# Top-k merge steps on TensorE moved to the front of their slot's tail and one slot later

## The chip, the cores and the metric

The kernel runs on one core of one Trainium2 chip. The metric is the device time of one execution in microseconds (us). The engines are named as in the profile: PE (TensorE, the matrix engine), PEld (its weight loads), DVE (VectorE), ACT (ScalarE), POOL (GpSimd) and SP (SyncE, which here issues transfers).

## The reference

The kernel computes attention with normalised queries and keys, then a mixture-of-experts layer in which each expert keeps at most its 80 best tokens.

```
q_n, k_n = rmsnorm(q, g_q), rmsnorm(k, g_k)      # q, k, v: 8 x 12 x 448 x 64
attn = softmax(q_n @ k_n.T / 8) ; x = (attn @ v) reshaped to 3584 x 768
probs = softmax(x @ w_gate)                      # 8 experts, one chosen per token
for e in experts:
    tokens = the (at most 80) tokens of expert e with the largest gate weight
    out[tokens] = gate_w * (relu(x[tokens] @ w1[e]) @ w2[e])   # others: zero
```

## The kernel before

**Tiling.** The 12 heads of a batch element are taken four at a time, so there are 24 groups of four heads, three to each of the eight batch elements b = 0 to 7. A group has seven rounds. One round is a score step (function `score`, L312: eight PE instructions, sixteen in the profile, into a PSUM tile `ps`), an exponential on ACT (L315, `ps` to `at`), and an attention-times-value step (`av`, L327, `at` into `po`). DVE adds up the seven `at` tiles of a group (`presum`, L339 and L341, tile `sm`).

**Order.** The order on every engine is written out by hand: the tile framework places semaphores and buffers, but moves nothing. Two rounds form a slot, and 84 slots (0 to 83) hold the attention. Each slot is emitted as: `begins`, the scores of two rounds, the presums of the two rounds before, `mid`, the AV steps of the two rounds before, then `end`. `begins`, `mid` and `end` are lists per slot, filled by `at_slot`, which appends. Every engine works through its own instructions strictly in that order.

**What else stands in a slot.** `end` holds the transposes of the next groups' normalised q and k (`transp`, L288, PE tile `tp`, copied by ACT in L300 and L302), the transposes of finished outputs (`xout`, L581, tile `xp`, copied by ACT into the single buffer `xb` in L586, then written to DRAM by SP in L593 and L594), and `rstd`. For q or k of a group, `rstd` is a DVE sum (L252) and scaling (L254) into `ms`, then a power on POOL (L261, `rs`). `normalise` in `mid` is POOL's multiplication L276 into `qn`, which `transp` reads. POOL also issues the staging copies of the expert weights (L175, L180).

**The merge.** When the three groups of a batch element are done, its gate is computed (L379 to L455), and then `merge` folds its 448 tokens into the running lists of the 80 best per expert, in six steps. Each step has PE work into a scratch tile `mp`, an ACT copy out of it, and mostly DVE work on the copy: `row` (L470, copy L474, then compares `beat`, L480 and L483), `experts` (L497, copy L501, more compares, `tied` L488 and L491), `own` (L506, copy L510, then `ahead` L514 and `cnt` L518), `counts` (L525 to L529, copies `back` L532 and `move` L534, then the chain `rnk`, `rank`, `put`, `keep`, L539 to L549), `place` (L557 and L561, copy L563) and `turn` (L567, copy L570). Batch elements 0 to 6 have a merge; the last one is handled behind the attention in its own code. The slot of a merge is given from b0 = (3b+2)*7//2, which is 7, 17, 28, 38, 49, 59 and 70.

**The buffers that matter.** `ps` and `mp` take turns in one pool of two PSUM buffers, so a merge step makes the next slot's second score step wait until ACT has copied `mp`:

```
scps = ps_stack.enter_context(tc.tile_pool(name="sc_ps", bufs=2, space=PSUM))
...
return scps.tile([128, 2, 512 if dt == F32 else 1024], dt, tag="sc", name="mp")
```

Of the kernel before, what the change touches and what calls it, by code (L numbers as in the profile page):

```python
# [20 lines left out]
def kernel(  # L21
# [15 lines left out]
    B, H, S, D = q.shape  # L37
# [168 lines left out]
    with av_stack:  # L206
# [406 lines left out]
        begins, mid, end = {}, {}, {}  # L613

        def at_slot(where, s, f, *a):
            where.setdefault(s, []).append((f, a))
# [9 lines left out]
        for g in range(NG):  # L626
            b0 = g * RD // 2
# [9 lines left out]
            for a in range(2):  # L637
                for f in range(2):
                    t = b0 - 4 + 2 * a + f
# [7 lines left out]
        for b in range(B):  # L647
            b0 = (NQ * b + NQ - 1) * RD // 2
            if b == B - 1:
                at_slot(end, b0 + 3, zl, b, range(NQ - 1))  # L650
                at_slot(end, b0 + 4, zl, b, range(NQ - 1, NQ))
                at_slot(end, b0 + 4, gate1, b)
                at_slot(end, b0 + 5, gate1t, b)
                at_slot(mid, b0 + 6, gate1v, b)
                continue
            at_slot(end, b0 + 5, zl, b, range(NQ))
            at_slot(end, b0 + 5, gate1, b)
            at_slot(end, b0 + 6, gate1t, b)
            at_slot(mid, b0 + 7, gate1v, b)
            at_slot(end, b0 + 7, gate2, b)  # L660
            at_slot(end, b0 + 7, gate2x, b)
            at_slot(mid, b0 + 8, gate2b, b)
            at_slot(mid, b0 + 8, gate2i, b)
            at_slot(mid, b0 + 8, gate2p, b)
            for t, fs in enumerate(merge(b)):
                for f in fs:
                    at_slot(end, b0 + 8 + t, f)
        at_slot(begins, 0, load_wgs)
        at_slot(end, NS - 3, weights_early)
        at_slot(end, NS, weights_late)  # L670
# [49 lines left out]
    b = B - 1  # L720
# [201 lines left out]
```

## Time and profile before

| what | value |
|---|---|
| median of three runs | 502.95 us (501.95 to 503.85) |
| the profiled execution itself | 498.67 us |
| its span, first to last instruction | 496.9 us |
| PE busy | 451.0 us, 91% |
| DVE busy | 358.0 us, 72% |
| ACT busy | 315.7 us, 64% |
| POOL busy | 267.7 us, 54% |
| mean granted PE clock | 0.978 of full speed |

The profile is of one execution, which was 4.28 us shorter than the median of the timed runs. Busy shares are means over a start of some 15 us, an attention of some 410 us and an expert stage of some 70 us, so they don't say which engine holds up the work at a given moment; for that one reads what an engine waited for, and where. A number in square brackets at the end of a row of a timeline is the idle time of that engine just before the row, with the instruction that ended it. The profile merges neighbouring rows of one kind and counts each fp32 matmul of 448 columns as two.

### The profile page before, as it was taken

To read this page: it belongs to the slowest core of one execution; us is meant where nothing else is said; L and a number is where in the kernel's file an instruction comes from. 1 tells how busy PE (TensorE), PEld (TensorE's weight loads), DVE (VectorE), ACT (ScalarE), POOL (GpSimd) and SP (SyncE) were. 2 spreads that over 40 slices of the span, in tenths; PEclk is the share of its full clock that TensorE was granted. 3 is DMA by queue.
4 is the path that set the end of the run, shared out by engine and by line. 5 is a ranking of instruction groups with operands and counts; after the bars stand their busy time and mean duration, and the time that the engine had idled before them with its cause. 6 is when DMAs were issued, how large, how long until landed. Compare 5 with 4: busy or idle time off the path is not lost. (4 is left out here: it accounts for less than half of the span.)

```text
span 496.9 us, 11200 instructions
## 1 busy us (share of the span) xinstructions
PE 451.0 (91%) x4527; PEld 222.3 (45%) x4527; DVE 358.0 (72%) x567; ACT 315.7 (64%) x491; POOL 267.7 (54%) x199
## 2 busy tenths in 40 slices
PE   6889999999899999699899999998998999869890
PEld 5334444353434444344344444443443444558770
DVE  4688756997899758776699669966976767445530
ACT  4777867877677768565787678767776666302210
POOL 2497883676555938618538835774578210242221
PEclk9799999999999999899999999999999999989996
DMA  6369979596958994994597959788939947779922
GB/s 217 117 136 300 254 184 251 97 291 183 243 121 222 230 256 74 267 162 159 172 167 247 254 166 241 188 218 200 238 98 220 211 90 264 281 214 354 372 98 60
DMA packets 68435, 100.84 MB, mean 203 GB/s; under 512 B 8480, under 2 KB 60192, under 8 KB 67104
## 3 DMA queue, kind: packets, MB, share of 16 engines
q1 hardware_dynamic: 52160, 70.54, 45.0%
q0 software_dynamic: 15616, 29.13, 32.9%
q8 instruction: 35, 0.57, 0.4%
q10 hardware_dynamic: 608, 0.46, 0.3%
q14 instruction: 16, 0.13, 0.1%
HBM read 101.12 MB, written 39.90 MB: 284 GB/s over the span
## 5 line engine op out<-in xcount | busy, mean ns | idle before, releaser
L261 POOL TENSOR_TENSOR rs<-ms,nhalf 128x14 f32<-128x14 f32 x46 | 136.5, 2970 | 130.2 <-DVE ms L254 124.0
L341 DVE TENSOR_TENSOR sm<-sm,at 128x896 f32<-128x896 f32 x120 | 155.6, 1297 | 24.1 <-ACT at L315 17.8
L315 ACT ACTIVATE at<-ps 128x896 f32<-128x896 f32 x168 | 147.8, 921 | 23.6 <-PE ps L312 19.2
L312 PE MATMUL ps<-qkT 64*64 64x448 f32 x1344 | 152.9, 561 | 9.6 <-ACT row L474 4.6
L327 PE MATMUL po<-at,vt 64*64 64x448 f32 x1344 | 145.4, 542 | 3.2 <-ACT us L332 3.2
L276 POOL TENSOR_TENSOR qn<-qk,rs 128x896 f32<-128x896 f32 (+1 forms) x45 | 84.5, 1894 | 8.3 <-DVE rs L267 8.2
L327 PEld LDWEIGHTS po<-at,vt 64*64 64x64 f32 x1344 | 50.2, 134 | 76.9 <-issue 67.0
L252 DVE TENSOR_REDUCE ms<-sq 128x14 f32<-128x896 f32 (+1 forms) x50 | 52.2, 1045 | 44.6 <-ACT sq L243 41.6
L312 PEld LDWEIGHTS ps<-qkT 64*64 64x64 f32 x1344 | 42.1, 134 | 73.7 <-issue 36.6
L288 PE MATMUL tp<-ident,qn 128*128 128x128 f32 x336 | 52.7, 280 | 5.1 <-DVE qn L276 3.5
L288 PEld LDWEIGHTS tp<-ident,qn 128*128 128x128 f32 x336 | 37.6, 142 | 32.0 <-issue 15.4
L586 ACT COPY xb<-xp 128x512 f32<-128x512 f32 x48 | 28.2, 588 | 36.6 <-PE xp L581 27.2
L243 ACT ACTIVATE sq<-qk 128x896 f32<-128x896 f32 (+1 forms) x50 | 45.9, 922 | 3.6 <-DMA qk<-in_k_dram 3.6
L581 PEld LDWEIGHTS xp<-ident,us 128*128 128x128 f32 x192 | 20.1, 140 | 34.7 <-issue 27.0
L300 ACT ACTIVATE qkT<-tp,gqk 128x512 f32<-128x512 f32 (+1 forms) x48 | 30.8, 643 | 4.7 <-PE tp L288 4.2
L302 ACT COPY qkT<-tp 128x384 f32<-128x384 f32 (+1 forms) x47 | 25.3, 538 | 12.0 <-PE tp L288 11.9
L581 PE MATMUL xp<-ident,us 128*128 128x128 f32 x192 | 31.5, 287 | 1.1 <-ACT xb L586 1.1
L863 ACT ACTIVATE h_sb<-ph 128x320 bf16<-128x320 f32 x16 | 7.0, 437 | 31.1 <-PE ph L859 31.1
L480 DVE TENSOR_SCALAR beat<-row,rg 128x128 bf16<-128x128 f32 (+3 forms) x28 | 23.2, 830 | 4.2 <-ACT row L474 3.8
L882 POOL DMA_INDIRECT out_dram<-yo,idxT x8 | 7.7, 963 | 34.2 <-DVE yo L877 14.9
L339 DVE TENSOR_TENSOR sm<-at 128x896 f32<-128x896 f32 x24 | 26.0, 1084 | 0.1
L332 ACT COPY us<-po 128x896 f32<-128x896 f32 x24 | 21.6, 902 | 5.8 <-PE po L327 5.8
(159 smaller groups left out, 407.9 us busy)
## 6 DMA issues: line engine op xcount, KB each, us to landing
wb_scratch<-in_moe_w_dram POOLq DMA_DIRECT2D x10, 1536.0 KB, 13.2
w_sb<-wb_scratch SPq DMA_DIRECT2D x10, 1536.0 KB, 11.1
vt<-in_v_dram SPq DMA_DIRECT2D x24, 448.0 KB, 6.1
out_dram<-zeros SPq DMA_DIRECT2D x28, 384.0 KB, 8.5
qk<-in_q_dram SPq DMA_DIRECT2D x23, 448.0 KB, 7.2
qk<-in_k_dram SPq DMA_DIRECT2D x23, 448.0 KB, 7.9
w_sb<-in_moe_w_dram POOLq DMA_DIRECT2D x6, 1536.0 KB, 15.3
xr_scratch<-xb SPq DMA_DIRECT2D x48, 192.0 KB, 5.5
```

The source lines that it names most:

```text
L243: nc.scalar.activation(st[g]["sq%d" % a][:, lo:hi], st[g]["qk"][a][:, lo:hi], AF.Square)
L252: nc.vector.reduce_sum(out=ms[:, lo:hi], in_=st[g]["sq%d" % a][:, lo:hi], axis=AX.X)
L261: nc.gpsimd.tensor_tensor(rs[:, lo:hi], ms[:, lo:hi], nhalf[:, lo:hi], op=ALU.pow)
L276: eng.tensor_mul(qn[:].rearrange("p (x hh) d -> p hh x d", hh=2)[:, h0:h1], qk[:, lo:hi].rearrange("p (hh x) d -> p hh x d", x=NX), rs[:, ...
L288: nc.tensor.transpose(tp[:, x * 128:(x + 1) * 128], qn[:, 2 * (x0 + x):2 * (x0 + x) + 2].rearrange("p h d -> p (h d)"), ident[:, :])
L300: nc.scalar.activation(o, i, AF.Copy, scale=gqk[:, :])
L312: nc.tensor.matmul(ps[u * 64:u * 64 + 64, hh, :S], T1[d, u, x * 64:(x + 1) * 64], T0[d, u, :], start=True, stop=True)
L315: nc.scalar.activation(at[:], ps[:, :, :S], AF.Exp)
L327: nc.tensor.matmul(po[hh * D:(hh + 1) * D, u, :S], vt[p, hh * NX + x, :], at[p, hh, :], start=(x == 0), stop=(x == RD - 1))
L341: nc.vector.tensor_add(s["sm"][:], s["sm"][:], s["at%d" % x][:])
L581: nc.tensor.transpose(xp[:, j * 128:(j + 1) * 128], us[:, u, c:c + 128], ident[:, :])
L586: nc.scalar.copy(xb[:, :, u * 128:(u + 1) * 128], xp[:, :].rearrange("p (j d) -> p j d", d=128))
```

## The change

For batch elements 0 to 5 each merge step goes to slot b0+9+t in place of b0+8+t, and it is put at the head of that slot's `end` list in place of its foot. The two or three parts of a step keep their order among themselves. The merge of batch element 6 stays as it was.

```
             for t, fs in enumerate(merge(b)):
-                for f in fs:
-                    at_slot(end, b0 + 8 + t, f)
+
+                ready = b < B - 2
+                for f in (reversed(fs) if ready else fs):
+                    if ready:
+                        end.setdefault(b0 + 9 + t, []).insert(0, (f, ()))
+                    else:
+                        at_slot(end, b0 + 8 + t, f)
```

On PE, around slots 15 and 16 (batch element 0), `row` (L470) stood between two slots, behind the output and q/k transposes:

```order
L327 MATMUL po<-at,vt 64x448 x8
L581 MATMUL xp<-ident,us 128x128 x4
L288 MATMUL tp<-ident,qn 128x128 x4
L470 MATMUL mp<-ident,rg 128x128 x4
L312 MATMUL ps<-qkT 64x448 x8
L327 MATMUL po<-at,vt 64x448 x8
L581 MATMUL xp<-ident,us 128x128 x4
L288 MATMUL tp<-ident,qn 128x128 x3
```

The same stretch of PE with the change:

```order
L327 MATMUL po<-at,vt 64x448 x8
L581 MATMUL xp<-ident,us 128x128 x4
L288 MATMUL tp<-ident,qn 128x128 x4
L312 MATMUL ps<-qkT 64x448 x8
L327 MATMUL po<-at,vt 64x448 x8
L470 MATMUL mp<-ident,rg 128x128 x4
L581 MATMUL xp<-ident,us 128x128 x4
L288 MATMUL tp<-ident,qn 128x128 x3
```

The step has moved behind a whole slot's scores and AV, and in front of that slot's transposes.

On DVE, at slots 18 and 19, where the chain behind `counts` stands; before:

```order
L341 TENSOR_TENSOR sm<-sm,at 128x896
L252 TENSOR_REDUCE ms<-sq 128x14
L254 TENSOR_SCALAR ms<-ms 128x14
L539 TENSOR_TENSOR rnk<-back,eq 128x32
L541 TENSOR_REDUCE rank<-rnk 128x4
L542 SCALAR_TENSOR_TENSOR rank<-rank,cnt 128x4
L545 TENSOR_TENSOR put<-iota,rank 128x320
L549 TENSOR_TENSOR keep<-iota,move 80x640
L339 TENSOR_TENSOR sm<-at 128x896
```

The same work on DVE with the change:

```order
L252 TENSOR_REDUCE ms<-sq 128x14
L254 TENSOR_SCALAR ms<-ms 128x14
L339 TENSOR_TENSOR sm<-at 128x896
L341 TENSOR_TENSOR sm<-sm,at 128x896
L539 TENSOR_TENSOR rnk<-back,eq 128x32
L541 TENSOR_REDUCE rank<-rnk 128x4
L542 SCALAR_TENSOR_TENSOR rank<-rank,cnt 128x4
L545 TENSOR_TENSOR put<-iota,rank 128x320
L549 TENSOR_TENSOR keep<-iota,move 80x640
```

Between the scaling of `ms` (L254), on which POOL's power waits, and the chain from `rnk` to `keep` there are now two presums. The orders of SP's and POOL's instructions are the same before and after.

## Rows read from the trace of the kernel before

**Rows 1.** Waits of PE: engine, tile, line, releaser: us in total, times, longest.
```profile
PE ps L312 <- ACT row L474: 4.6, 6, 0.9
PE ps L312 <- ACT move L534: 4.2, 2, 4.0
```

**Rows 2.** Timeline of PE, batch element 0: start, us, engine, line, instruction.
```profile
86.09 0.62 PE L470 MATMUL mp<-ident,rg 128*128 128x128 f32 x4 [0.17 <-DVE eqb L431]
86.64 0.98 PE L312 MATMUL ps<-qkT 64*64 64x448 f32 x8
88.49 0.98 PE L312 MATMUL ps<-qkT 64*64 64x448 f32 x8 [0.87 <-ACT row L474]
89.30 1.68 PE L327 MATMUL po<-at,vt 64*64 64x448 f32 x16
...
92.15 1.92 PE L312 MATMUL ps<-qkT 64*64 64x448 f32 x16
93.89 1.68 PE L327 MATMUL po<-at,vt 64*64 64x448 f32 x16
...
100.32 0.24 PE L525 MATMUL mp<-eqb,beat 128*128 128x8 bf16 x4
...
101.46 1.86 PE L312 MATMUL ps<-qkT 64*64 64x448 f32 x16
...
106.21 1.74 PE L312 MATMUL ps<-qkT 64*64 64x448 f32 x16
107.76 1.68 PE L327 MATMUL po<-at,vt 64*64 64x448 f32 x16
109.38 0.98 PE L288 MATMUL tp<-ident,qn 128*128 128x128 f32 x7
```

**Rows 3.** Timeline of PE, batch element 1.
```profile
138.10 0.98 PE L312 MATMUL ps<-qkT 64*64 64x448 f32 x8 [0.65 <-ACT row L474]
...
163.05 0.66 PE L288 MATMUL tp<-ident,qn 128*128 128x128 f32 x4
```

**Rows 4.** Timeline of DVE, batch element 0.
```profile
93.36 2.57 DVE L483 TENSOR_SCALAR beat<-row,rg 128x64 bf16<-128x64 f32 x1
...
101.60 1.08 DVE L341 TENSOR_TENSOR sm<-sm,at 128x896 f32<-128x896 f32 x1
...
103.71 0.17 DVE L254 TENSOR_SCALAR ms<-ms 128x14 f32<-128x14 f32 x1
...
104.43 0.49 DVE L545 TENSOR_TENSOR put<-iota,rank 128x320 bf16<-128x320 f32 x1
104.84 0.81 DVE L549 TENSOR_TENSOR keep<-iota,move 80x640 bf16<-80x640 f32 x1
```

**Rows 5.** Timeline of POOL, batch element 0.
```profile
103.96 2.59 POOL L261 TENSOR_TENSOR rs<-ms,nhalf 128x14 f32<-128x14 f32 x1 [0.33 <-DVE ms L254]
106.52 1.69 POOL L276 TENSOR_TENSOR qn<-qk,rs 128x896 f32<-128x896 f32 x1
```

**Rows 6.** Timeline of POOL, batch element 1.
```profile
157.48 3.36 POOL L261 TENSOR_TENSOR rs<-ms,nhalf 128x14 f32<-128x14 f32 x1 [1.37 <-PE ps L312]
160.81 1.68 POOL L276 TENSOR_TENSOR qn<-qk,rs 128x896 f32<-128x896 f32 x1
```

**Rows 7.** Timeline of PE, batch element 2.
```profile
208.41 1.76 PE L312 MATMUL ps<-qkT 64*64 64x448 f32 x8 [4.03 <-ACT move L534]
```

**Rows 8.** Timeline of ACT, batch element 2.
```profile
207.06 0.58 ACT L586 COPY xb<-xp 128x512 f32<-128x512 f32 x1 [4.12 <-DMA xr_scratch<-xb]
```

**Rows 9.** Timeline of SP and of POOL, batch element 2: issues of transfers.
```profile
194.41 1.48 SPq L593 DMA_DIRECT2D xr_scratch<-xb  x2
...
193.23 0.90 POOL L180 DMA_DIRECT2D wb_scratch<-in_moe_w_dram  x1
```

**Rows 10.** Busy time in windows (us), PE, PEld, DVE, ACT, POOL, granted clock, DMA.
```profile
208.40:211.00 2.60, 2.59 (x16) 1.08 (x20) 2.50 (x4) 1.55 (x2) 2.60 (x3) 0.52 0.70 251
```

**Rows 11.** Timeline of DVE, batch element 2.
```profile
210.19 1.94 DVE L545 TENSOR_TENSOR put<-iota,rank 128x320 bf16<-128x320 f32 x1
```

## The prediction

> **What bounds the kernel now.** I read the busy shares first (PE 91%, no other engine over 72%), then what PE waited for, then timelines around the longest of those waits. The list of PE's waits is headed by score steps that wait for a merge step's ACT copy: 4.6 us in six waits for `row`, 4.2 us in two for `move` [rows 1]. The reader is to see that there are six of the first kind, one per merge of batch elements 0 to 5, and that one single wait makes up nearly all of the second. The timelines alternate by batch element: the even ones (0, 2, 4) wait 0.87 us [rows 2], the odd ones (1, 3, 5) 0.65 us [rows 3]. Outside these places PE works through the slots of the attention almost without a pause, so what is taken off PE there is taken off the time, unless another engine then arrives late. The engine to watch is POOL: its multiplication `qn` feeds the q/k transposes, and it lies behind DVE's `ms`, on the engine where the merge's DVE parts stand.
>
> **The waits that go.** A pair of score steps normally takes 1.55 us to the AV steps behind it (107.76 − 106.21). In the slot behind `row` it takes 2.66 us (89.30 − 86.64), 1.11 us more, and behind `experts` 1.74 us (93.89 − 92.15), 0.19 us more [rows 2]. The cause is the pair of buffers that `ps` and `mp` share: with the step at the foot of a slot, its copy stands on ACT behind the slot's `xb` and `qkT` copies, and the second score step needs that buffer. At the head of `end` the copy stands in front of those two, and PE still has the transposes and one score step to do before it needs the buffer. I therefore take these waits as gone. For an even batch element that is 0.17 (`row` waiting for DVE) + 1.11 + 0.19 + about 0.15 for `counts`, an estimate from the 0.19: 1.6 us. For an odd one it is 0.65 + 0.24 (the part of 1.11 that the profile doesn't book as waiting) + 0.19 + twice 0.15 for `own` and `counts`: 1.4 us. PE's own instructions are the same ones, so they cost nothing new. The six slots' copies on ACT are only reordered; ACT's exponentials lie beside PE's AV and transposes.
>
> **What limits the gain.** PE can run ahead only as far as `qn` allows. Even: POOL's first `qn` ends at 106.52 + 1.69 = 108.21 [rows 5], and the four transposes that read it are the last four of the seven that start at 109.38, so about 109.8 [rows 2]: 1.6 us of slack. Odd: 160.81 + 1.68 = 162.49 [rows 6] against 163.05 [rows 3]: 0.56 us.
>
> How does that chain move? Up to the second scaling of `ms` in question the same instructions stand on DVE in both orders, since each compare, presum and reduction only changes places with its neighbour; DVE is busy there without a pause, so its sum stays. Three things differ:
> - POOL's power took 2.59 us when small operations of the merge followed the scaling on DVE [rows 5], and 3.36 us when presums followed [rows 6]. The new order puts presums there in the even elements: 0.77 us later. In the odd ones presums stand there already: 0.
> - In the even elements the chain from `rnk` to `keep` now stands behind two presums. From 103.79, right behind the start of the scaling [rows 4], two presums of 1.1 us and 0.64 us of `rnk` and `rank` (104.43 − 103.79) lead to `put` 2.85 us later, `keep` 3.26 us later and `keep`'s end 4.07 us later (0.41 = 104.84 − 104.43, and 0.81). The power ends 3.36 + 0.17 = 3.53 us after that point, so `qn` finds `keep` running and starts 0.5 us late.
> - In the old order compares were caught behind POOL's multiplications; the worst took 2.57 us [rows 4], some 2.2 us more than a compare that isn't caught. In the new one the compares start one slot later, and a presum and a compare meet the same multiplications, for 1.69 us each at most. Laying the rows end to end by hand I get DVE 0.8 us earlier in the even and 0.4 us earlier in the odd elements; the bounds are 0 and 2.2 us.
>
> Even: 1.6 − 0.77 − 0.5 + 0.8 = 1.1 us of room, less than the 1.6 saved; I take 1.0 for semaphores on the way. Odd: 0.56 + 0.4 = 0.96, less than 1.4; I take 0.9. Without the third point it is 0.3 and 0.56, with more of it the full 1.6 and 1.4. So the regular part is 3 × 1.0 + 3 × 0.9 = 5.7 us, bounds 2.6 and 9.0. `ahead`, `put` and `keep` come in time for their PE steps by my replay, by 0 to 1 us: if DVE is that much later, PE waits there instead of at the transposes, within the same bounds.
>
> **The one long stall.** In batch element 2 ACT's copy into `xb` waited 4.12 us for the previous group's write [rows 8]: issued at 194.41, 1.2 us behind a staging copy of weights [rows 9], it had landed only at 207.06. PE waited 4.03 us [rows 7], for the `move` copy queued behind `xb` on ACT, and then ran 2.6 us at half clock, 0.52 of full speed [rows 10], 1.2 GHz in place of 2.4, which cost about 1.3 us more. Price: 5.3 us. With the change PE has, at that point, one more score step and two AV steps that need nothing of ACT; it stops only at `counts`, for a buffer whose exponential stands behind `xb` on ACT. If the write takes the same 207.06 − 194.41 = 12.65 us from an issue 1.3 us earlier (0.17 + 1.11 saved by then), ACT resumes at 205.8 and PE at about 207.7, behind `xb`, `qkT` and one exponential (an estimate of 1.9 us). That is 0.7 us earlier than 208.41, with a score step of 0.78 (half of 1.55), AV steps of 1.62 (109.38 − 107.76) and 1.3 us of slow clock behind it, but `counts`, some 1.0 us (101.46 − 100.32 = 1.14, a little waiting in it), ahead of it [rows 2]: 0.7 + 0.78 + 1.62 + 1.3 − 1.0 = 3.4 us, of which 1.0 is counted as regular. That leaves 2.4 us, or 1.1 if the clock falls again; 5.3 if the write lands in time, for which it speaks that POOL's staging copy is now issued behind it (the power in front of it takes 0.77 us more). I take 2.4, since the only row of this transfer is that of 12.65 us.
>
> **Sum.** 5.7 + 2.4 = 8.1 us off the profiled execution (498.67 us, span 496.9 us). The timed median is 4.28 us above that execution for a reason that the profile can't show; I carry the difference over unchanged: 502.95 − 8.1 = 494.85, say 494.8 us. Own range of this case: 2.6 + 1.1 = 3.7 to 9.0 + 5.3 = 14.3 us, so 488.7 to 499.2 us.
>
> **Rivals.**
> - POOL's chain takes it all. The waits on `row` go, but the transposes wait for `qn` as long as the merge's DVE work comes a slot later, and the stall stays, because earlier PE work only reaches the write of `xb` sooner. For it speak the slack of 0.56 us; against it that in the even elements there are 1.6 us. It gives 0 to 3 us: 501.5 us.
> - Slower: `put` and `keep` land behind POOL's two multiplications in the even elements. Where that happened, `put` took 1.94 us in place of 0.49 [rows 11, 4]. If `qn` starts first, `put` waits out one multiplication and `keep` the second, 1.69 us each plus their own 0.41 and 0.81, so `keep` ends 4.6 us after `put`'s issue, some 4 us after PE wants it for `place`, which is now at the head of `end` with the transposes behind it. Against 1.6 us gained by then an even element loses 2.4 us. Three of them cost 7.2, the odd ones still give 2.7, the stall nothing: 4.5 us slower, 507.5 us. It decides by what comes first: `put` at 2.85 and `keep` at 3.26 us against `qn` at 3.53. With a power of 2.59 us, `qn` would start at 2.76 and win. That a presum follows the scaling is what speaks against it. The Trainium skill says in "SBUF — State Buffer", Who interferes with whom, that a VectorE instruction with two SBUF inputs and a GpSimd instruction that reads SBUF exclude each other, whichever is issued first holding the port to its end. By that rule this rival is the outcome if the order of issue tips; the trace agrees with the rule in the 1.94 us.
> - Everything goes: no chain binds and the `xb` write lands in time, 14.3 us: 488.7 us. For it speaks only that the staging copy moves behind the write.
>
> **How the numbers follow.** Forecast 0.55, everything goes 0.14, POOL's chain takes it all 0.18, slower 0.13. About 0.5% (2.5 us) is what a measurement of this kernel tells from no change. Faster: 0.55 + 0.14 and a quarter of the third case, some 0.74. Same: the rest of that case, 0.14. Slower: 0.12. The range 489.5 to 503.0 us leaves out the slower case and the far end of the all-goes case, and holds the third whole.
>
> **What would show it.** Right: no PE wait for `row` but for batch element 6; score steps of 1.55 us behind each merge step; the odd elements' transposes waiting some 0.5 us for `qn` on POOL; POOL's powers of 3.36 us in the even elements. Wrong: PE waiting at `place` (L557, L561) for `put` or `keep`, or at `counts` for `ahead`, or a stall of 3 us or more behind an `xb` copy in places where there was none; or a `row` wait that survives, which would say that ACT, not the place in the queue, was late.

## The result, and the profile after

The changed kernel takes 490.79 us (median of 4 runs, 490.19 to 491.93) against 503.4 us before (4 runs, 501.95 to 504.59): a ratio of 0.9753, 95% interval 0.9721 to 0.9786. The forecast was 494.8 us. The profiled execution took 490.89 us, its span is 489.0 us, 7.9 us less than the span before.

In the page of the changed kernel, the first line of part 1 gives busy time, share of the span and instructions. PE's busy time is 3.2 us less and POOL's 18.2 us more, though both issue the same instructions as before.

```profile
PE 447.8 (92%) x4527; PEld 224.5 (46%) x4527; DVE 353.7 (72%) x567; ACT 314.6 (64%) x491; POOL 285.9 (58%) x199
```

The list of PE's waits, to be held against [rows 1]:

```profile
PE tp L288 <- POOL qn L276: 8.0, 9, 2.5
...
PE mp L525 <- ACT at L315: 0.4, 1, 0.4
...
PE ps L312 <- ACT own L510: 0.2, 1, 0.2
```

Both rows of [rows 1] are gone: no score step waits for `row` or `move` any more. In their place the q/k transposes wait for POOL's `qn`. One of the nine waits, the longest (2.5 us), lies at the start of the program; eight, 5.5 us together, lie beside the merges.

In the timelines of PE a row of L312 marked x16 is the two score steps of a slot (one score step is four PE instructions, eight in the profile). The timeline of PE for batch element 0, against [rows 2]; the score steps behind `row` (L470) take 94.00 − 92.44 = 1.56 us, where it was 2.66:

```profile
91.10 0.65 PE L470 MATMUL mp<-ident,rg 128*128 128x128 f32 x4
...
92.44 1.73 PE L312 MATMUL ps<-qkT 64*64 64x448 f32 x16
94.00 1.68 PE L327 MATMUL po<-at,vt 64*64 64x448 f32 x16
...
109.10 0.33 PE L557 MATMUL mp<-info,put 128*80 128x40 bf16 x4
109.28 0.46 PE L561 MATMUL mp<-listn,keep 80*80 80x5 bf16 x8
109.59 0.53 PE L288 MATMUL tp<-ident,qn 128*128 128x128 f32 x3
111.44 0.66 PE L288 MATMUL tp<-ident,qn 128*128 128x128 f32 x4 [1.32 <-POOL qn L276]
```

`place` (L557, L561) waits for nothing; the four transposes behind it stand 1.32 us for `qn`. Where that comes from is to be read on POOL and DVE, first the timeline of POOL (against [rows 5]), then that of DVE (against [rows 4]):

```profile
101.87 3.39 POOL L261 TENSOR_TENSOR rs<-ms,nhalf 128x14 f32<-128x14 f32 x1 [3.10 <-DVE ms L254]
...
105.23 3.14 POOL L261 TENSOR_TENSOR rs<-ms,nhalf 128x14 f32<-128x14 f32 x1
108.35 3.04 POOL L276 TENSOR_TENSOR qn<-qk,rs 128x896 f32<-128x896 f32 x1
```

```profile
104.76 0.17 DVE L254 TENSOR_SCALAR ms<-ms 128x14 f32<-128x14 f32 x1
104.84 1.08 DVE L339 TENSOR_TENSOR sm<-at 128x896 f32<-128x896 f32 x1
105.96 1.09 DVE L341 TENSOR_TENSOR sm<-sm,at 128x896 f32<-128x896 f32 x1
...
107.61 0.49 DVE L545 TENSOR_TENSOR put<-iota,rank 128x320 bf16<-128x320 f32 x1
108.02 0.81 DVE L549 TENSOR_TENSOR keep<-iota,move 80x640 bf16<-80x640 f32 x1
108.76 1.08 DVE L341 TENSOR_TENSOR sm<-sm,at 128x896 f32<-128x896 f32 x1
```

`qn` takes 3.04 us where it took 1.69. It is issued at 108.35, while `keep` runs (to 108.83). Counted back from its end, 108.35 + 3.04 − 1.69 = 109.70, it got going only about when the presum behind `keep` was done (108.76 + 1.08 = 109.84). So two DVE instructions in a row went ahead of it, one of them issued after it. This is so all nine times that it meets `keep` and a presum in three profiles of the new order (after, after_again and a_xb2: 3.04 to 3.11 us).

It is not so behind every pair. Earlier in the same merge a multiplication met two presums, of which the first ran until 94.57; here it got in behind the first, and the second one, issued 0.69 us after it, stood for it (2.46 us in place of 1.08). POOL, then DVE:

```profile
93.92 2.20 POOL L276 TENSOR_TENSOR qn<-qk,rs 128x896 f32<-128x896 f32 x1
...
94.61 2.46 DVE L341 TENSOR_TENSOR sm<-sm,at 128x896 f32<-128x896 f32 x1
```

The rows show one difference: the second presum reads the `sm` that the first writes, and starts 0.04 us behind its end, while the presum behind `keep` reads nothing of `keep` and starts 0.07 us before its end (108.76 against 108.83). Whether that decides it was not tried.

The second place to look is ACT's wait for the write of `xb`, from the list of ACT's waits. Before:

```profile
ACT xb L586 <- DMA xr_scratch<-xb: 7.4, 2, 4.1
```

and after:

```profile
ACT xb L586 <- DMA xr_scratch<-xb: 1.3, 1, 1.3
```

There had been two stalls and not one: besides that of [rows 8] another of 3.3 us in the slots of batch element 6. Both are gone; the 1.3 us are at another place, in batch element 4. The timelines of SP and POOL for batch element 2 in the changed kernel show the issue of the write and that of the staging copy, against [rows 9]:

```profile
193.93 1.24 SPq L593 DMA_DIRECT2D xr_scratch<-xb  x2
...
194.88 0.91 POOL L180 DMA_DIRECT2D wb_scratch<-in_moe_w_dram  x1
```

The staging copy now stands 0.95 us behind the write, where it stood 1.2 us ahead of it, and the next copy into `xb` waits for no transfer.

**Where the time went.** The merges of the first six batch elements lie in slots b0+8 to b0+14. This table gives the time from the first score step of slot b0+8 to that of slot b0+15, as read from PE's timeline of each kernel (from the third on they are those of the experiments), with the sum over the six:

```
us, merge of batch element      0     1     2     3     4     5     sum
before                       32.47 33.00 38.04 32.92 32.11 33.19  201.73
after                        32.07 32.11 32.51 31.88 32.01 32.91  193.49
after, profiled again        32.07 32.10 34.20 31.88 32.00 32.92  195.17
before, second xb buffer     32.43 33.07 32.18 32.92 32.11 32.93  195.64
after, second xb buffer      33.83 32.18 32.58 31.94 32.08 32.98  195.59
after, earlier qn            31.13 31.77 31.07 31.77 30.91 32.04  188.69
before, both edits           32.81 32.93 32.10 32.93 32.11 32.93  195.81
after, both edits            31.19 31.78 31.14 31.78 30.30 31.78  187.97
```

Between the two profiles the merges give 8.24 us, of it 38.04 − 32.51 = 5.53 in element 2 alone, and slot 75 (the stall of element 6) 9.99 − 7.63 = 2.36 us. Against this the changed execution began its first score step 2.35 us later (17.05 us for 14.70); the rest is within 0.7 us. The two sums of the new order that stand near 195.6 (profiled again, and second xb buffer) each hold one merge that is 1.7 us longer (34.20 and 33.83), in which TensorE's clock fell behind a short wait; the last section shows it.

### The profile page after: what moved, and what is told of

Same layout as the page of the kernel before. It is cut to its first block, busy times and chain, and to the rows that moved or that the text cites. A ratio compares the mean times of both kernels' runs of the same rounds, so it can differ in the third digit from the quotient of the medians.

```text
span 489.0 us, 11182 instructions
## 1 busy us (share of the span) xinstructions
PE 447.8 (92%) x4527; PEld 224.5 (46%) x4527; DVE 353.7 (72%) x567; ACT 314.6 (64%) x491; POOL 285.9 (58%) x199
## 5 line engine op out<-in xcount | busy, mean ns | idle before, releaser
L261 POOL TENSOR_TENSOR rs<-ms,nhalf 128x14 f32<-128x14 f32 x46 | 146.5, 3188 | 104.8 <-DVE ms L254 100.6
L341 DVE TENSOR_TENSOR sm<-sm,at 128x896 f32<-128x896 f32 x120 | 169.0, 1408 | 22.2 <-ACT at L315 16.5
L315 ACT ACTIVATE at<-ps 128x896 f32<-128x896 f32 x168 | 145.7, 922 | 17.4 <-PE ps L312 17.4
L312 PE MATMUL ps<-qkT 64*64 64x448 f32 x1344 | 147.8, 553 | 1.1 <-DVE qkT L298 0.9
L276 POOL TENSOR_TENSOR qn<-qk,rs 128x896 f32<-128x896 f32 (+1 forms) x45 | 92.1, 2062 | 10.2 <-DVE rs L267 10.1
L312 PEld LDWEIGHTS ps<-qkT 64*64 64x64 f32 x1344 | 43.8, 133 | 62.3 <-issue 44.2
L879 PE MATMUL py<-w_sb,h_sb 128*80 128x384 bf16 x128 | 23.1, 332 | 1.8 <-ACT h_sb L868 1.8
```

Of the source, the lines that this page charges most:

```text
L261: nc.gpsimd.tensor_tensor(rs[:, lo:hi], ms[:, lo:hi], nhalf[:, lo:hi], op=ALU.pow)
L276: eng.tensor_mul(qn[:].rearrange("p (x hh) d -> p hh x d", hh=2)[:, h0:h1], qk[:, lo:hi].rearrange("p (hh x) d -> p hh x d", x=NX), rs[:, ...
L312: nc.tensor.matmul(ps[u * 64:u * 64 + 64, hh, :S], T1[d, u, x * 64:(x + 1) * 64], T0[d, u, :], start=True, stop=True)
L315: nc.scalar.activation(at[:], ps[:, :, :S], AF.Exp)
L341: nc.vector.tensor_add(s["sm"][:], s["sm"][:], s["at%d" % x][:])
```

## Experiments

The theory after this reading: nearly all of the gain is ACT's stalls behind the single `xb` buffer, which the new order happens to avoid; the merge's new place itself gives little, because the waits it saves come back as waits for `qn`. The rival: the gain is the saved `row` and `counts` waits, as most of the forecast's sum had it. The runs fall into three groups, each with its own runs of the kernel before: 500.17 us (25 runs) for the first four, 500.82 us (13 runs) for the next four, 501.27 us (11 runs) for the last three.

**again: the kernel before, unchanged.**

```
(no edit)
```

> The kernel before, unchanged, to see why its timed runs are 4 to 5 us longer than the profiled one (498.67 us) while the changed kernel's timed and profiled runs agree (490.8 and 490.89 us). First theory: the time is lost in stalls of ACT behind the write of xb, which vary from run to run; then this profile, if it is at about 503 us, shows three or four xb copies that waited 2 us or more for a transfer, against two (7.4 us in total) in the profile shown, and the same waits for row (4.6 us in six). Rival: the loss is spread, at the start or in the expert stage, and the xb waits are the same two.

Measured: 499.97 us (496.5 to 504.03), ratio 0.9989 (0.9949 to 1.0029). The list of ACT's waits:

```profile
ACT xb L586 <- DMA xr_scratch<-xb: 6.3, 2, 3.4
```

The stalls come back at the same two places, with other lengths (2.9 and 3.4 us). This profiled execution took 500.69 us, 2.0 us more than the first one, with 1.1 us less of waits for the write: these two profiles do not bear out that the stalls make the spread. The kernel before spreads over 6.6 us in 24 of these 25 runs (496.6 to 503.16; one took 504.62), the changed one over 1.7 in its four.

**head: the merge steps at the head of `end`, but in their old slot.**

```
-                        end.setdefault(b0 + 9 + t, []).insert(0, (f, ()))
+                        end.setdefault(b0 + 8 + t, []).insert(0, (f, ()))
```

> One part of the change alone: the merge steps of batch elements 0 to 5 go to the head of their slot's end list, but stay in their old slot (b0+8+t). First theory (both parts are needed, the slot later makes the operands ready): the waits of 0.87 and 0.65 us on the row copy go, but PE waits about 1.2 us at L470 for DVE's rg and eqb, and the merge's DVE work now stands ahead of rstd, so the transposes wait for qn some 1 to 2 us more per merge: 498 to 505 us, no gain. Rival (the place in the slot is all that counts): 491 to 494 us.

Measured: 498.64 us (496.83 to 500.5), ratio 0.9976 (0.9951 to 1.0001). PE's waits:

```profile
PE tp L288 <- POOL qn L276: 10.1, 9, 2.3
...
PE mp L470 <- DVE eqb L431: 2.4, 2, 1.2
```

The head of the list alone removes the `row` waits and both stalls (ACT has no wait for the write), but `row` now comes before the gate's DVE work is done, and the transposes wait longer. The merges take 202.08 us in sum: 6.4 us over the 195.64 of the old order without stalls (second xb buffer in the table), so what the stalls give is lost again there. The first theory held, in the time and in the wait of 1.2 us at L470.

**later: one slot later, at the foot.**

```
-                    at_slot(end, b0 + 8 + t, f)
+                    at_slot(end, b0 + 8 + t + (b < B - 2), f)
```

> The other part alone: the merge steps of batch elements 0 to 5 go one slot later (b0+9+t), but stay at the foot of their slot's end list. First theory (the place on ACT behind xb and qkT is what makes row wait, and the slot later alone only removes the 0.17 us wait of L470): row still makes the second score step wait 0.65 to 0.87 us six times, and the xb stall in batch element 2 stays or not by the timing of its transfer: 499 to 503 us. Rival (the slot later is what helps): 491 to 495 us, without the row waits.

Measured: 499.95 us (498.19 to 502.38), ratio 1.0003 (0.9975 to 1.0032). PE's waits:

```profile
PE ps L312 <- ACT own L510: 3.9, 6, 1.8
...
PE tp L288 <- POOL qn L276: 3.8, 2, 3.0
```

and of ACT's:

```profile
ACT xb L586 <- DMA xr_scratch<-xb: 5.3, 2, 4.1
```

The time is the one expected, the waits are not: no score step waits for `row`; the wait for a merge copy has moved to `own`. Of the stalls only that of batch element 6 stays (4.1 us); in batch element 2 ACT no longer waits for the write, and a wait of 1.2 us stands in batch element 4. Neither half of the change gives anything alone that these runs resolve; only the two together do.

**a_qn: the changed kernel, with POOL's first multiplication of a pair one slot earlier.**

```
-                    at_slot(mid, b0 - 5 + a + min(late, 2), normalise, g, a)
+                    at_slot(mid, b0 - (5 if a or g == 1 else 6) + a + min(late, 2), normalise, g, a)
```

> The changed kernel with POOL's multiplication for q of groups 2 to 23 one slot earlier (b0-6 in place of b0-5), so that it stands in front of the power for k and not behind it. First theory (in the changed kernel the chain of power and qn on POOL sets when the transposes start, and takes back most of what the row waits give): the nine waits of the transposes on POOL (8.0 us) shrink to under 2 us and the time falls by 4 to 6 us, to 485 to 487 us. Rival (the waits only change their name: put and keep or the compares on DVE are caught behind the multiplication, and PE waits at place or counts): 489 to 492 us.

Measured: 484.41 us (483.15 to 485.79), ratio 0.9696 (0.9643 to 0.9749), 0.6 us under the lower end of what was expected. In PE's waits `tp` no longer waits for `qn` on POOL at all. POOL's timeline shows the multiplication between the two powers, and each within 2.2 us:

```profile
103.87 2.13 POOL L276 TENSOR_TENSOR qn<-qk,rs 128x896 f32<-128x896 f32 x1
105.97 3.43 POOL L261 TENSOR_TENSOR rs<-ms,nhalf 128x14 f32<-128x14 f32 x1
109.48 1.82 POOL L276 TENSOR_TENSOR qn<-qk,rs 128x896 f32<-128x896 f32 x1
```

So the chain through `qn` held back 193.49 − 188.69 = 4.80 us of the changed kernel's gain in the merges, by the profiles. The medians differ by 6.4 us (490.79 − 484.41); in the profiles the rest lies before the first score step (15.80 us for 17.05) and behind the attention (0.8 us), and that the chain caused it is not shown.

**b_xb2: the kernel before, with a second `xb` buffer.** Four tiles share buffers with others to make room: `lx` and `keep` those of `own`, and in the same way (left out below) `ahead` and `put` those tagged `cand`. The order of every engine stays.

```
-            lx = gpool.tile([128, NT, H, E], F32, tag="lx", name="lx", bufs=1)
+            lx = tpool.tile([128, NT, H, E], F32, tag="own", name="lx")
...
-                m["keep"] = tpool.tile([CAP, E, CAP], BF16, tag="keep", name="keep")
+                m["keep"] = tpool.tile([CAP, E, CAP], BF16, tag="own", name="keep")
...
-                st[g]["xb"] = prep.tile([128, NJ + 1, 256], F32, tag="xb", name="xb", bufs=1)
+                st[g]["xb"] = prep.tile([128, NJ + 1, 256], F32, tag="xb", name="xb", bufs=2)
```

> The kernel before with two buffers for xb in place of one (the room comes from sharing tags: keep and the gate's products with own; ahead and put with cand), in the same order on every engine. First theory (stalls of ACT behind the write of xb, in batch elements 2 and 6, are most of what the change won): both stalls go, the slots 40 and 75 fall from 9.3 to 10.6 and from 10.0 to 11.5 us to about 4.8 and 7.6, and the time falls by 6 to 8 us, to 492 to 494 us where before runs at 500. Rival (the write is late because the DMA engines are full, and with a second buffer something else waits for them): 498 us or more.

Measured: 491.3 us (490.02 to 492.54), ratio 0.9796 (0.9763 to 0.9829), 9.5 us below the kernel before, where 6 to 8 were expected. Both stalls are gone: slot 40 took 4.73 us and slot 75 7.63, as the first theory had it. PE's waits:

```profile
PE ps L312 <- ACT row L474: 4.6, 6, 0.9
```

This is the run that decides. The old order, with all its `row` waits, is as fast as the new one once ACT need not wait for the write.

**a_xb2: the changed kernel with the same second buffer**, the same edit as in b_xb2.

> The changed kernel with the same two buffers for xb. First theory (the change has already lost the xb stalls but for one of 1.3 us): within 1 us of the changed kernel, and 2 to 4 us faster than the kernel before with two buffers, which is then what the order of the merge steps is worth by itself. Rival (the order of the steps is worth what the timed difference says): 8 to 12 us faster than the kernel before with two buffers.

Measured: 491.81 us (490.25 to 493.12), ratio 0.981 (0.9775 to 0.9845): within 1 us of the changed kernel, as expected, but not the expected 2 to 4 us faster than the old order with two buffers. The two long stalls were already gone, sharing buffers costs nothing that shows, and PE's waits stay about as they were:

```profile
PE tp L288 <- POOL qn L276: 8.5, 9, 2.0
```

**after_again: the changed kernel, unchanged**, in the same group.

> The changed kernel, unchanged, beside the kernel before in the same runs, since the kernel before spreads over 8 us from run to run (496.5 to 504.6). First theory (a stall of ACT behind xb that comes and goes makes that spread, and the first timing happened to meet slow ones): 489 to 492 us with a spread under 3 us, some 9 us below the kernel before. Rival (the 12.6 us of the first timing is the change's own): 487 to 489 us.

Measured: 491.63 us (490.21 to 493.12), ratio 0.98 (0.9763 to 0.9837). Old order with two buffers, new order with two and new order with one: 491.3, 491.8 and 491.6 us. The difference that the order makes here is smaller than what these runs resolve; in the profiles it is 195.64 − 193.49 = 2.15 us over the six merges for the first profile of the changed kernel, 0.47 us for the second (195.17) and 0.05 us with the second buffer (195.59). The changed kernel lies 9.2 us below the runs of the kernel before in this group, as the first theory said; the 12.6 us of the first timing were measured against runs at 503.4 us.

**b_qn: the kernel before with the earlier multiplication**, the edit of a_qn.

> The kernel before with POOL's multiplication for q one slot earlier, as the control for the same edit on the changed kernel, which won 6.4 us there. First theory (before, the transposes don't wait for qn, so it gives nothing; it only moves the slots by what DVE and POOL block of each other): within 2 us of the kernel before. Rival (the edit is good by itself, whatever the merge does): 493 to 495 us.

Measured: 505.55 us (501.02 to 508.79), ratio 1.0099 (1.006 to 1.0137): 1% slower, which neither theory had. The profile is of the fastest of its ten runs. ACT's waits:

```profile
ACT xb L586 <- DMA xr_scratch<-xb: 13.8, 6, 4.5
```

The same edit that gives the new order 6 us costs the old one 5: six copies into `xb` stall in place of two. That POOL's staging copies, which stand behind the multiplication, have moved against SP's writes is the likely reason: in groups 3 to 20 seven writes are now issued 0 to 3.9 us behind a staging copy, and land 9.7 to 12.3 us later, where it was five before. It was not tried by itself.

**best: the changed kernel with both edits**, second buffer and earlier multiplication.

> The new order with both disturbances taken out: two buffers for xb, so that ACT never waits for the previous write, and POOL's multiplication of the next q one slot earlier, so that no transpose waits for it. The theory that the merge's order is worth its row waits, but only where neither the xb write nor POOL's qn sets the pace: 482 to 484.5 us, at most 2.5 us under the new order with the earlier multiplication alone (484.4), because that run had only 2.7 and 1.5 us of xb waits left. No row wait, no xb wait, no tp wait for qn on POOL. The rival, that the second xb buffer is worth several us by itself wherever it stands: 478 to 480 us.

Measured: 481.86 us (480.1 to 482.61), ratio 0.9617 (0.9573 to 0.966). It beats both kernels and lies just under the expected 482 to 484.5; the rival's 478 to 480 did not come. What is left of the merge in PE's waits:

```profile
PE mp L561 <- DVE keep L549: 0.8, 2, 0.4
...
PE mp L557 <- DVE put L545: 0.5, 2, 0.3
```

With POOL out of the way the next thing to be late is the DVE chain behind `place`, by tenths.

**b_xb2_qn: the kernel before with both edits.**

> The old order of the merge with the same two edits. Theory (the order is worth its row and counts waits, 1.4 to 1.6 us a merge, once nothing else binds): the row waits (4.6 us in six) stay, the transposes have no wait on qn either way, so the earlier multiplication brings nothing here: 490 to 492 us, 7 to 9 us above the new order with both edits. Rival (the order of the merge is worth nothing, and the earlier multiplication helps either order): 483 to 486 us, within 1.5 us of the new order with both.

Measured: 488.73 us (486.81 to 490.81), ratio 0.976 (0.9714 to 0.9807), 6.9 us above the last. PE's waits:

```profile
PE ps L312 <- ACT row L474: 4.6, 6, 0.9
```

So the order is worth 6.9 us where nothing else binds, 195.81 − 187.97 = 7.84 us in the merges by the profiles, and about nothing where `qn` binds. The median came out 1.3 us under the expected 490 to 492. The theory had left out the start: from the first score step to slot 15 the profile took 64.65 us against 66.96 in b_xb2, because the one long wait of the transposes for `qn` at the start (2.8 us there) is gone too. Within the merges the earlier multiplication gave the old order nothing (195.81 against 195.64).

**a_nokeep: the changed kernel, in which the merges behind the first reuse element 0's `keep`.**

```
+        kept = []
...
+                if b:
+                    m["keep"] = kept[0]
+                    return
                 m["keep"] = tpool.tile([CAP, E, CAP], BF16, tag="keep", name="keep")
+                kept.append(m["keep"])
```

> The new order, but the merges of batch elements 1 to 5 (and 6) don't compute their keep tile; they use that of element 0 (this part of the computation is left out). Element 0 is the control in the same run. Theory (in the even elements POOL's qn comes 0.5 to 1 us late because keep and then a presum stand before it on DVE, back to back, and POOL gets in only behind both): in elements 2 and 4 the first qn takes about 2.4 us in place of 3.04 (it then waits for the presum alone), the transposes there wait 0.6 us less than in element 0, and the whole is 1 to 2 us faster than the new order: 489 to 491 us. Rival (keep is not in the way; the presum alone holds POOL, or the power is late): qn and the waits as in element 0, and the time that of the new order, 490.8 to 491.6 us.

Measured: 487.34 us (486.99 to 490.59), ratio 0.9747 (0.9701 to 0.9793); that interval overlaps after_again's, so the time alone does not settle it. The median lies 1.7 us under the expected 489 to 491; leaving `keep` out also takes its 0.81 us off DVE in every merge behind the first, and the odd ones came out 0.1 to 0.7 us shorter too. What settles the question is the profile. POOL's timeline, first element 0, the control, then element 2:

```profile
107.91 3.04 POOL L276 TENSOR_TENSOR qn<-qk,rs 128x896 f32<-128x896 f32 x1
...
209.00 2.31 POOL L276 TENSOR_TENSOR qn<-qk,rs 128x896 f32<-128x896 f32 x1
```

and DVE's in element 2:

```profile
208.27 0.49 DVE L547 TENSOR_TENSOR put<-iota,rank 128x320 bf16<-128x320 f32 x1
208.68 1.08 DVE L341 TENSOR_TENSOR sm<-sm,at 128x896 f32<-128x896 f32 x1
```

Without `keep` the multiplication has only the rest of one presum in front of it (to 209.76; 209.00 + 2.31 − 1.69 = 209.62) and takes 2.31 us in elements 2 and 4, as against the expected 2.4; in the changed kernel it took 3.04 in all three even elements. The wait of the transposes there fell with it, from 1.38 to 0.64 us in element 2, while in element 0 it stayed at 1.32.

The timed runs, by order of the merge and by what else was changed (us, median):

```
                              old order      new order
one xb buffer                 500 to 503     491 to 492
second xb buffer                491.3          491.8
earlier qn                      505.6          484.4
both                            488.7          481.9
```

## Why the prediction was right, and where it was not

The time came out 4 us under the forecast and in the range. Those 4 us are the difference between profile and median, which was carried over. From profile to profile the forecast took off 8.1 us and 7.8 came off (498.67 to 490.89), but that is luck: two errors of opposite sign, and a start that came out 2.35 us later. The regular part was sized 5.7 us and measured 2.15 at the most (0.47 and 0.05 in the other two profiles); the stall was sized 2.4 us and measured about 8, at two places.

**The waits that go: right.** No wait on `row` is left, and the score steps behind the merge steps take 1.50 to 1.62 us against the 1.55 forecast; only behind `own` in the odd elements they still take 1.75, 1.75 and 2.03. The gross saving, forecast as 1.6 us (even) and 1.4 us (odd), 9.0 in all, is shown by the two kernels with both edits: 1.62, 0.96 and 1.81 us in the even and 1.15 us in each odd merge, 7.84 in all.

**What limits the gain: the right chain, with one term too small.** Transposes wait for `qn`, as said, and the powers in the even elements come to 3.12 to 3.39 us (forecast 3.36). The three steps of the sum for an even element can be laid beside element 0, with times counted from the first score step of slot 15 (81.66 us before, 83.74 after):
- `ms` is scaled 1.03 us earlier (103.71 − 81.66 = 22.05, now 104.76 − 83.74 = 21.02); forecast 0.8. Right.
- The second power ends at 24.61 where it ended at 24.86: 0.25 us earlier instead of 1.03, so 0.78 us are lost, as forecast (0.77). The parts differ: 0.55 are its own length, and 0.23 are that the power before it, now 3.39 us long, still occupied POOL.
- "`qn` finds `keep` running and starts 0.5 us late": this is the step that failed. `keep` did end 0.48 us after `qn`'s issue, but the presum behind it went first, and `qn` ran 1.35 us longer than 1.69. With it the room is 1.6 − 0.78 − 1.35 + 1.03 = 0.5 us, and element 0 gained 0.4; the forecast had 1.1 and took 1.0.

In elements 2 and 4 another 0.6 and 0.3 us of waiting for `qn` came one group earlier. Against the old order with two `xb` buffers, the three even merges gained 0.1 us together (forecast 3.0), the odd ones 2.0 (forecast 2.7): 1.0 each in elements 1 and 3, nothing in element 5, where the transposes wait 0.79 us for `qn` and a score step 0.24 for `own`. The forecast 0.5 us of waiting for `qn` in the odd elements was 0.26, none and 0.79. The rival that POOL's chain takes it all was therefore right for the even elements and wrong for the stall.

The Trainium skill, "SBUF — State Buffer", Who interferes with whom, has a two-input VectorE instruction and a GpSimd read exclude each other, with the right of way by order of issue. The exclusion agrees with 3.04 and 2.31 us. The order of issue does not, by the starts in the profile: `qn` started at 108.35 and stood behind a presum that started at 108.76. The measurement decides here: a waiting POOL instruction can be passed by DVE's next one, as behind `keep`, and need not be, as between the two presums at 93.49 and 94.61.

**The one long stall: mis-sized, and not the only one.** "I take 2.4, since the only row of this transfer is that of 12.65 us" chose the wrong end. The write was not as long again: with the staging copy issued behind it, which the forecast had noted and weighed too little, it took 4.2 us (9.2 in the second profile, where ACT waited 0.3 us), and the whole stall went, 38.04 − 32.18 = 5.86 us against the old order's undisturbed merge (the forecast's upper end was 5.3). The second stall, of 3.3 us in element 6, was missed altogether: there PE waited in the gate's and the output's steps and not in a score step, so the rows for `row` and `move` did not show it. It gave 2.36 us. ACT's wait row, 7.4 us in two, would have shown both.

**Carried over unchanged: wrong.** The 4.28 us by which the median stood above the profiled execution were not a constant; the changed kernel's profiled execution lies at its median. The kernel before spreads over 6.6 us in 24 of its 25 runs, those with two buffers over 2.5 to 4 in four or six each; that the stalls make part of that spread is likely, with so few runs not shown. Part of it goes with TensorE's clock: of the 25 runs the shortest (496.6 us) had a mean granted clock of 0.984 and the longest (504.62 us) one of 0.967, with a correlation of −0.54 over all.

**The slower rival** did not come about: `put` (0.49 us) and `keep` (0.81 us) ran unhindered, `keep` was issued 0.33 us before `qn`, and no wait at `place` shows. The margin was a third of a microsecond. **Everything goes** (488.7 us) was right on the stall and wrong on the chain.

What stays open is why the write is long in some places. In four profiles (before, again, after, a_qn), worked out from issues and landings of groups 3 to 20, the eleven writes issued 0.4 to 4.1 us behind a staging copy landed 10.1 to 12.6 us after their issue, and the eighteen with a staging copy 0.9 to 6.3 us behind them within 4.2 to 7.7 us. Two with the staging copy 0.4 and 0.7 us behind them took 9.0 and 9.3 us, two issued 5.2 us behind one 9.7 and 9.9, and writes with none near 3.7 to 9.0. The other nine profiles show the first half again (22 writes issued at most 4.1 us behind a staging copy: 9.3 to 12.8 us) and soften the second: with the staging copy 0.9 to 6.3 us behind them 36 writes took 4.0 to 9.6 us, and some with none near up to 11.3. So a staging copy just ahead went with a long write each time, but isn't the only thing that makes one long, and no run moved a staging copy alone.

## What to carry to other kernels

Read the list of waits of every engine before sizing a stall, and not PE's alone: a copy that waits for its buffer's previous write shows whole on its own engine and in scattered, small waits elsewhere. Before an instruction is counted as hidden or as late by the rest of one other, look at what the other engine runs right behind it. And when a reordering gains, give the old order a second buffer as a control: here it gained the same, and the reordering paid only once the chain through `qn` was shortened too.

## What was not expected of the hardware

- POOL's multiplication, ready during one DVE instruction, was passed over for a second: 3.04 us, with the control of 2.31 us where only one stood ahead of it. Between two presums, of which the second needs the first, it was not passed over (2.20 us).
- A wait of 1.40 us was followed by half the clock in one run and one of 1.32 us at the same place was not in another. In the changed kernel with the second buffer, PE's timeline and then the windows (us; busy time of PE, PEld, DVE, ACT, POOL; granted clock; DMA) show a clock of 0.50 (1.2 GHz):

```profile
111.15 0.66 PE L288 MATMUL tp<-ident,qn 128*128 128x128 f32 x4 [1.40 <-POOL qn L276]
111.73 3.21 PE L312 MATMUL ps<-qkT 64*64 64x448 f32 x16
```

```profile
112.00:114.00 2.00, 2.00 (x16) 0.58 (x12) 1.90 (x2) 0.98 (x2) 1.59 (x1) 0.50 1.10 347
```

  and the same stretch of the changed kernel one of 1.00 (2.4 GHz):

```profile
111.40:114.00 2.60, 2.56 (x28) 1.28 (x32) 2.50 (x2) 1.56 (x3) 2.48 (x1) 1.00 1.09 352
```

  It is the 33.83 us in the table of merges, 1.8 us over the changed kernel's 32.07. The length of the wait does not decide it: in batch element 2 of the changed kernel a wait of 1.38 us was followed by a clock of 1.00 (214 to 217 us), and in its second profile one of 1.37 us by 0.51 (the 34.20 us, 1.7 us over 32.51). Short waits on PE can thus cost more than their length, and not in every run.
- A write of the same size to memory landed after 3.7 to 12.6 us in groups 3 to 20 of four profiles; it was long each time that it was issued up to 4.1 us behind a staging copy.
